# Clustered attention and two FFNs: the sums of v and of the weights in other products, b's abs at another place, a new order

## The chip, the cores and the metric

The kernel runs on one core of one Trainium2 chip. TensorE is PE here, its weight loads PEld, VectorE is DVE, ScalarE ACT, GpSimd POOL, and SyncE SP; SPq is SP's own queue, on which it issues DMAs. The metric is the device time of one execution in microseconds; the median over the runs is the time of a kernel.

## The reference

```python
q_n, k_n, c_n = q / (|q| + 1e-6), k / (|k| + 1e-6), centroids / (|centroids| + 1e-6)
q_assign = argmax(einsum('bhsd,hcd->bhsc', q_n, c_n)); k_assign = the same with k_n
scores = q @ k.T / sqrt(D), and -1e9 where q_assign != k_assign
attn = exp(scores - max); attn = attn / (sum(attn) + 1e-9)
x = (attn @ v) as 1536 tokens of 512
h = x @ w_in;  g = softplus(h);  x = g @ w_out             # first FFN, 512 -> 2048 -> 512
h = x @ w_in;  g = P(h) / (Q(h) + 1e-6);  out = g @ w_out  # second FFN
P = a0 + a1 h + a2 h^2 + a3 h^3;  Q = 1 + |b0| |h| + |b1| h^2
```

There are 2 batches, 8 heads, 768 positions, heads of 64 and 16 clusters. Everything is float32.

## The kernel before

**Attention.** A batch and two heads make a pair; there are eight pairs, 0 to 7. The two heads of a pair lie in one tile. `dots` (L231) multiplies x, which holds q and k, by the centroids, transposes on DVE (L237), and `onehot1` and `onehot2` (L244 to L255) find the best cluster. `mask_rows` scales the one-hot on ACT (L260) and SP moves it by eight DMAs of 16x384 into rows of the operands `qt` and `kt` (L148), so that the product of the scores has the mask in it. `split1` to `split4` cut q and k into a high and a low part, on ACT and DVE and with DMAs. `maxes` (L277, L281) are the products for the row maxima, twelve per pair, each reduced on DVE into a column of `mf`; `max_rows` (L289, L291) transposes `mf` on PE (`nt`), and a DMA puts the negated maxima into `qt` as one more row (`nr`). Then `scores` (L321, L322) makes twelve tiles `st` of 128 keys for 768 queries, ACT takes the exponential into `et` (L326), and from the second key tile on, POOL adds `et` up in `ea` (L331). `av` (L343) multiplies by v; `sums` (L366) multiplies `ea` by ones, so that every row of a head's 64 holds the sum; `evac_sums` and `finish` (L375 to L396) make the reciprocal with Ln, Exp and one correction on DVE, multiply and split the result into `xh` and `xl`. Since the mask leaves equal terms in rows, a small share of the sum of v is taken away: `vsum1` (L300) reduces v over the key tiles on DVE, `vsum2` (L306, L309) sums over partitions on PE (`vt`) into `nv`, the bias of `evac_av` (L357).

**Banks.** PSUM has three rotating bank pairs from `bank()`, for `st`, `mxs`, `dt`, `nt`, `vt` and `sm`, and one pair for `av`.

**Order.** `step(j)` issues the scores of pair j, the maxes of j+1, dots and splits of j+2 and the rest of j-1. The order on all engines comes from tables of positions: `AT` for a steady step, `S0` and `M0` for step 0, `LEAD` for what lies ahead of it, `DE` for the weight decode in steps 6 and 7, `FT` for the start of the FFN and the decode in the second. Functions are called in the sequence of their positions, and each engine works in that order.

**FFNs.** A unit is one chunk of 128 hidden features for 512 tokens: 12 products for h (L497 to L499) and 12 for yp (L568 to L574), each of three terms of a high and low split; 16 chunks, 3 blocks and 2 FFNs make 96 units. A weight chunk is decoded in five pieces: three on DVE (L429, L435, L441), a cast on ACT (L447), a subtraction on DVE (L450). The polynomial runs on ACT and DVE (L516 to L539), `gh` and `gl` are the two parts of its result, and the outputs `yo` leave PSUM by copies shared between DVE and ACT (L596, L597). `b_sb` holds b; its absolute value is taken in the lead (L678).

## Time and profile before

| | us |
|---|---|
| median of 3 runs (lowest to highest) | 816.33 (814.92 to 818.18) |
| the profiled execution, and its span | 817.65, 815.9 |
| PE busy in the span | 774.9 (95%) |
| DVE, ACT, POOL busy | 596.7, 443.2, 186.6 |
| the chain that ended last | PE 73%, DVE 15%, ACT 7%, DMA 2% |
| first score of pair 0, first `gl` product of the FFN | 46.55, 276.41 |

A row of a timeline gives the start in us, the duration, engine, line, operation, output and inputs, tile and count, and in brackets the idle time ahead of it and what released it. A window's row gives busy time of each engine with counts, then the granted clock of TensorE as a share of full speed, the DMA share and GB/s. The sums (`sm`) of pairs 4, 5, 6 and 7 begin at 185.8, 214.9, 245.1 and 267.1.

### The profile page before, as it was taken

The numbers are of one execution on the slowest core, as the hardware profiler recorded it, in microseconds if no ns is written. First come the engines' busy times: TensorE is split into PE (matmuls) and PEld (weight loads), VectorE is DVE, ScalarE is ACT, GpSimd is POOL, SyncE is SP. The second block draws the span as 40 slices with busy tenths as digits, with TensorE's granted clock in tenths as the row PEclk, the third lists the DMA queues.
The fourth block names the chain that finished last, engine by engine and source line by source line (L and its number), as shares of the span: only waits on it lengthen the run. The fifth ranks groups of instructions, "written<-read, shape, count | busy, mean of one in ns | idle before, by whom it ended". The sixth has DMA issues, their size and how long they took to land.

```text
span 815.9 us, 9120 instructions
## 1 busy us (share of the span) xinstructions
PE 774.9 (95%) x3468; PEld 573.9 (70%) x3468; DVE 596.7 (73%) x760; ACT 443.2 (54%) x626; POOL 186.6 (23%) x103
## 2 busy tenths in 40 slices
...
GB/s 185 166 46 128 132 146 81 112 125 62 123 71 239 320 41 1 104 0 1 1 1 0 104 197 171 200 104 0 1 1 0 52 1 0 1 0 53 1 1 51
DMA packets 14635, 61.65 MB, mean 76 GB/s; under 512 B 3248, under 2 KB 4368, under 8 KB 10496
## 3 DMA queue, kind: packets, MB, share of 16 engines
...
q8 instruction: 27, 0.44, 0.2%
...
## 4 chain that ended last, share of the span: by engine, by line
PE 73%; DVE 15%; ACT 7%; DMA 2%; issue 1%; POOL 1%; SPq 0%; ACTq 0%; POOLq 0%; DVEq 0%
PE h L498 9%; PE h L499 9%; PE h L497 9%; PE av L343 7%; PE yp L569 5%; PE yp L570 5%; PE yp L568 5%; PE st L321 4%; PE yp L572 4%; PE yp L573 4%; PE yp L574 4%; PE st L322 3%; PE mxs L277 3%; ACT et L326 2%; DVE y L531 2%; DVE y L539 2%
## 5 line engine op out<-in xcount | busy, mean ns | idle before, releaser
L498 PE MATMUL h<-xl,w 128*128 128x512 f32 x384 | 151.9, 396 | 0.0
L499 PE MATMUL h<-xh,w 128*128 128x512 f32 x384 | 151.8, 395 | 0.0
L497 PE MATMUL h<-xh,w 128*128 128x512 f32 x384 | 151.6, 395 | 0.0
L331 POOL TENSOR_TENSOR ea<-ea,et 128x768 f32<-128x768 f32 x60 | 118.3, 1989 | 26.0 <-ACT et L326 23.9
L553 DVE TENSOR_TENSOR gl<-y,gh 128x512 fp32r<-128x512 f32 x48 | 33.1, 690 | 116.7 <-ACT gh L545 116.7
L510 ACT ACTIVATE y<-h 128x512 f32<-128x512 f32 x48 | 28.8, 599 | 154.0 <-PE h L499 154.0
L281 DVE TENSOR_REDUCE mf<-mxs 128x1 f32<-128x768 f32 x96 | 87.7, 950 | 33.8 <-PE mxs L277 32.8
L326 ACT ACTIVATE et<-st 128x768 f32<-128x768 f32 x96 | 73.4, 812 | 71.1 <-PE st L322 68.1
L497 PEld LDWEIGHTS h<-xh,w 128*128 128x128 f32 x384 | 72.1, 188 | 17.9 <-issue 0.6
L498 PEld LDWEIGHTS h<-xl,w 128*128 128x128 f32 x384 | 72.1, 188 | 17.4
L499 PEld LDWEIGHTS h<-xh,w 128*128 128x128 f32 x384 | 72.0, 188 | 17.3
L572 PE MATMUL yp<-w,gh 128*128 128x512 f32 x192 | 75.7, 394 | 4.3 <-ACT gh L547 2.3
L569 PE MATMUL yp<-gl,w 128*128 128x512 f32 x192 | 76.9, 400 | 2.9 <-DVE gl L553 2.9
L568 PE MATMUL yp<-gh,w 128*128 128x512 f32 x192 | 76.5, 399 | 1.4 <-issue 1.4
L570 PE MATMUL yp<-gh,w 128*128 128x512 f32 x192 | 76.5, 399 | 0.0
L573 PE MATMUL yp<-w,gl 128*128 128x512 f32 x192 | 75.8, 395 | 0.5 <-DVE gl L555 0.5
L574 PE MATMUL yp<-w,gh 128*128 128x512 f32 x192 | 75.5, 393 | 0.0
L343 PE MATMUL av<-et,vr 128*64 128x384 f32 x384 | 73.0, 508 | 1.0 <-ACT et L326 1.0
L321 PE MATMUL st<-qt,kt 128*128 128x384 f32 x192 | 70.7, 368 | 2.8 <-DVE mf L281 2.1
L322 PE MATMUL st<-qt,kt 81*128 81x384 f32 x192 | 65.9, 343 | 0.0
L277 PE MATMUL mxs<-kt,qt 80*128 80x384 f32 x192 | 52.9, 385 | 11.3 <-DMA kt<-mr 4.8
L321 PEld LDWEIGHTS st<-qt,kt 128*128 128x128 f32 x192 | 36.8, 192 | 24.8 <-DVE mf L281 7.1
...
## 6 DMA issues: line engine op xcount, KB each, us to landing
...
rawx<-in_x SPq DMA_DIRECT2D x7, 768.0 KB, 6.5
rawy<-in_y SPq DMA_DIRECT2D x7, 768.0 KB, 6.4
...
```

Of the source, the lines that this page charges most:

```text
L321: nc.tensor.matmul(t[:, n, 0:HS], lhsT=KT[j % 3][:, 0, h, c], rhs=QT[j % 3][:, 0, h, r], start=True, stop=False)
L331: eng.tensor_tensor(out=ea[j, h], in0=et[j, 0, h] if kt == 1 else ea[j, h], in1=e, op=ALU.add)
L343: nc.tensor.matmul(av_t[j][64 * h:64 * h + 64, n, 0:HS], lhsT=VR[j % 2][:, h, kt, :], rhs=et[j, kt, h][:, n, :], start=kt == 0, stop=kt == ...
L497: nc.tensor.matmul(t, lhsT=wh[:, kk, :], rhs=h, start=kk == 0, stop=False)
L498: nc.tensor.matmul(t, lhsT=wh[:, kk, :], rhs=l, start=False, stop=False)
L499: nc.tensor.matmul(t, lhsT=wl[:, kk, :], rhs=h, start=False, stop=kk == KD - 1)
L568: nc.tensor.matmul(t, lhsT=wh[:, s], rhs=gh, start=first, stop=False)
L569: nc.tensor.matmul(t, lhsT=wh[:, s], rhs=gl, start=False, stop=False)
L570: nc.tensor.matmul(t, lhsT=wl[:, s], rhs=gh, start=False, stop=last)
L572: nc.tensor.matmul(t, lhsT=gh[:, s], rhs=wh, start=first, stop=False)
L573: nc.tensor.matmul(t, lhsT=gl[:, s], rhs=wh, start=False, stop=False)
L574: nc.tensor.matmul(t, lhsT=gh[:, s], rhs=wl, start=False, stop=last)
```

## The change

1. `vsum1` and `vsum2` are gone. A tile of `et` has one more column of ones; the value product of the second half has 385 columns, and the sum of v comes out in the last, which `evac_av` reads as its bias. `et` has eight fixed tiles instead of six that rotate.
2. The sums are taken in four column tiles of 32, in two rounds: first `ea`, then directly the last key tile, which POOL no longer adds. The reciprocal works on 384 columns instead of 768, and eight DMAs of 32x384 on SP spread it into `rr`.
3. `dots` multiplies by the raw centroids, which arrive transposed as one more input `ct`; an ACT activation (`scaled`) applies the reciprocal norm `rn`. The transpose on PE and the scaled copy are gone; the plain centroids come in eight small DMAs.
4. The absolute value of b is taken at step 2, and the DMAs of a and b are issued after both heads' maxima of pair 0.
5. All tables of positions are new, and the lead and step 0 are sorted as one sequence with a table of its own, `A0`. The load of the next x and y moves to the end of a step. At the start of the FFN one h group stands ahead of the last value product, and two stand between the last sums and the first yp; before, it was two and one.
6. In the second FFN the polynomial's `qr` has its own two buffers, all `yo` of blocks 0 and 1 are copied on ACT, the first yp of blocks 1 and 2 comes a unit later, and the decode of chunks 14 and 15 is spread out.

```diff
-AT = dict(S=[[0.31, 0.59, 2.52, 2.92, 2.56, 5.1], [0.23, 0.9, 2.82, 3.36, 2.83, 3.41]],
+AT = dict(S=[[0.28, 0.44, 2.19, 3.3, 2.6, 1.85], [0.2, 0.25, 2.53, 3.17, 2.8, 3.59]],
...
-    A=[-0.02, 0.22, 1.25], L=[0.26, 0.77, 1.61], D2=[[51.2, 51.8, 52.2, 52.4, 52.8], [56.2, 56.8, 57.2, 57.4, 57.8]])
+    A=[0.25, 1.03, 2.14], L=[0.86, 2.1, 2.52], D2=[[49.6, 51.0, 52.6, 53.15, 54.2], [55.5, 56.8, 58.2, 59.15, 59.5]])
...
+    ET = [ap_.tile([128, S + 1], F32, name=f"et{s}") for s in range(NE)]
...
-        nc.vector.transpose(t, d[:, 0, 0:HS])
+        nc.scalar.activation(out=u, in_=d[:, 0, 0:HS], func=AF.Identity, scale=rn[:, j % PB:j % PB + 1])
+        nc.vector.transpose(t, u)
...
-    def vsum1(j):
...
-    def vsum2(j):
...
     def scores(j, kt, h):
...
-        if kt:
+        if 0 < kt < NT - 1:
...
     def av(j, kt):
...
-                    av_t[j][64 * h:64 * h + 64, n, 0:HS], lhsT=VR[j % 2][:, h, kt, :], rhs=et[j, kt, h][:, n, :],
-                    start=kt == 0, stop=kt == NT - 1,
+                    av_t[j][64 * h:64 * h + 64, n, 0:HS + n], lhsT=VR[j % 2][:, h, kt, :],
+                    rhs=et[j, kt, h][:, n * HS:(n + 1) * HS + n], start=kt == 0, stop=kt == NT - 1,
...
-        nc.scalar.activation(out=t, in_=av_t.pop(j)[:, :, 0:HS], func=AF.Identity, scale=-1.0, bias=NV[j % 2])
+        p = av_t.pop(j)
+        nc.scalar.activation(out=NV[j % 2], in_=p[:, 1, HS:HS + 1], func=AF.Copy, scale=EPS / S)
+        nc.scalar.activation(out=t, in_=p[:, :, 0:HS], func=AF.Identity, bias=NV[j % 2])
...
     def sums(j):
...
-        for n in range(2):
+        for x in range(2):
             for h in range(2):
-                nc.tensor.matmul(
-                    t[64 * h:64 * h + 64, n, 0:HS], lhsT=ones, rhs=ea[j, h][:, n, :], start=True, stop=True
-                )
+                src = ea[j, h] if x == 0 else et[j, NT - 1, h]
+                for n in range(2):
+                    g = 32 * (2 * h + n)
+                    nc.tensor.matmul(
+                        t[g:g + 32, 0, 0:HS], lhsT=ones[:, 0:32], rhs=src[:, n * HS:(n + 1) * HS], start=x == 0, stop=x == 1
+                    )
...
-            nc.vector.scalar_tensor_tensor(out=r0, in0=w0, scalar=-2.0, in1=r0, op0=ALU.add, op1=ALU.mult)
+            nc.vector.scalar_tensor_tensor(out=r0, in0=w0, scalar=2.0, in1=r0, op0=ALU.add, op1=ALU.mult)
+            for h in range(2):
+                for n in range(2):
+                    g = 32 * (2 * h + n)
+                    for r in (64 * h, 64 * h + 32):
+                        nc.sync.dma_start(out=w[r:r + 32, n, :], in_=r0[g:g + 32, :])
         elif part == 3:
-            nc.vector.tensor_tensor(out=a, in0=a, in1=r0, op=ALU.mult)
+            nc.vector.tensor_tensor(out=a, in0=a, in1=w, op=ALU.mult)
...
-        qr = pools["wa"].tile([128, 2, TB], F32, tag="w32", name="qr", bufs=3)
+        qr = pools["wa"].tile([128, 2, TB], F32, tag="qr", name="qr", bufs=2)
...
-        nc.scalar.copy(y, t) if i % 2 else nc.vector.tensor_copy(y, t)
+        nc.scalar.copy(y, t) if i % 2 or blk < NB - 1 else nc.vector.tensor_copy(y, t)
...
-            nc.vector.scalar_tensor_tensor(out=b_sb, in0=b_sb, scalar=-1.0, in1=b_sb, op0=ALU.mult, op1=ALU.max)
...
-            for _, _, fn in sorted(seq, key=lambda x: x[:2]):
+            for _, _, fn in sorted(seq + lead, key=lambda x: x[:2]):
...
         for j in range(NP - 1):
+            if j == 2:
+                nc.vector.scalar_tensor_tensor(out=b_sb, in0=b_sb, scalar=-1.0, in1=b_sb, op0=ALU.mult, op1=ALU.max)
...
-            put(F1 + 0.8 + 0.01 * (i - F1) if F1 - 2 <= i < F1 else i + (1 + (c == 0), 3)[f] + 0.9, o)
+            put(F1 + 0.8 + 0.01 * (i - F1) if F1 - 2 <= i < F1 else i + (1 + (c == 0), 3 + (c == 0 and blk > 0))[f] + 0.9, o)
```

The order at three places. First DVE at the end of the lead, before; `mf_111` are the maxima of pair 0, `mf_112` those of pair 1, `nr` the negated maxima:

```order
L255 STREAM_TRANSPOSE oh<-turned 128x384
L281 TENSOR_REDUCE mf_111<-mxs 128x1 x4
L678 SCALAR_TENSOR_TENSOR b_sb<-b_sb 128x2
L281 TENSOR_REDUCE mf_111<-mxs 128x1
L291 TENSOR_SCALAR nr<-nt 6x128
L281 TENSOR_REDUCE mf_112<-mxs 128x1 x2
```

The same place of the changed kernel, where `mf_114` and `mf_115` are the maxima of pairs 0 and 1:

```order
L287 TENSOR_REDUCE mf_114<-mxs 128x1
L258 TENSOR_REDUCE dmx<-turned 128x24
L259 TENSOR_TENSOR turned<-iota,dmx 128x384
L261 STREAM_TRANSPOSE oh<-turned 128x384
L287 TENSOR_REDUCE mf_114<-mxs 128x1 x4
L297 TENSOR_SCALAR nr<-nt 6x128
L287 TENSOR_REDUCE mf_115<-mxs 128x1 x2
```

The absolute value of b no longer stands among the maxima.

Second SP's queue in a steady step, before; `mr` are mask rows, `nr` the maxima's row, `qt` and `kt` the operands:

```order
L148 DMA qt_105<-nr 1x12x128
L145 DMA vr_110<-in_v 128x768
L148 DMA kt_107<-qt_104 16x1536
L148 DMA kt_107<-qt_104 48x1536
L148 DMA kt_107<-kt_107 64x1536
L148 DMA qt_104<-qt_104 16x1536
L140 DMA rawx<-in_x 128x1536
L140 DMA rawy<-in_y 128x1536
L148 DMA qt_104<-mr 16x384 x2
L148 DMA kt_107<-mr 16x384 x2
```

The same queue of the changed kernel, from one `nr` to the mask rows behind it:

```order
L152 DMA qt_100<-nr 1x12x128
L144 DMA rawx<-in_x 128x1536
L144 DMA rawy<-in_y 128x1536
L149 DMA vr_113<-in_v 128x768
L152 DMA kt_102<-qt_99 16x1536
L152 DMA kt_102<-qt_99 48x1536
L152 DMA qt_99<-qt_99 16x1536
L418 DMA rr<-r_869 32x384 x8
L152 DMA kt_102<-kt_102 64x1536
L152 DMA qt_99<-mr 16x384 x2
L152 DMA kt_102<-mr 16x384 x2
```

The loads of x and y now stand right behind `nr`, and the eight DMAs of the reciprocal stand ahead of the last key copy and the mask rows.

Third DVE in step 6, before; `mf_112` are the maxima of pair 7, and `w` the pieces of the first weight chunk:

```order
L291 TENSOR_SCALAR nr<-nt 12x128
L281 TENSOR_REDUCE mf_112<-mxs 128x1 x4
L429 TENSOR_SCALAR w_1790<-w_1770 128x1024
L435 SCALAR_TENSOR_TENSOR w_1790<-w_1770,w_1790 128x1024
L281 TENSOR_REDUCE mf_112<-mxs 128x1 x2
L441 SCALAR_TENSOR_TENSOR w_1790<-w_1770,w_1790 128x1024
L300 TENSOR_REDUCE vs<-vr_110 128x128
L281 TENSOR_REDUCE mf_112<-mxs 128x1
L450 TENSOR_TENSOR w_1849<-w_1790,w_1849 128x1024
```

The same step of the changed kernel, where `mf_115` are pair 7's maxima:

```order
L297 TENSOR_SCALAR nr<-nt 12x128
L287 TENSOR_REDUCE mf_115<-mxs 128x1 x8
L411 TENSOR_TENSOR sm<-sm,r_1799 128x384
L413 SCALAR_TENSOR_TENSOR r_1799<-sm,r_1799 128x384
L287 TENSOR_REDUCE mf_115<-mxs 128x1 x3
L420 TENSOR_TENSOR avs<-avs,rr 128x768
L287 TENSOR_REDUCE mf_115<-mxs 128x1
L459 TENSOR_SCALAR w_1932<-w_1759 128x1024
L297 TENSOR_SCALAR nr<-nt 12x128
L465 SCALAR_TENSOR_TENSOR w_1932<-w_1759,w_1932 128x1024
L471 SCALAR_TENSOR_TENSOR w_1932<-w_1759,w_1932 128x1024
```

All twelve maxima of pair 7 now precede the first piece of a weight.

## Rows read from the trace of the kernel before

**Rows 1.** Windows: a steady step, three slow stretches, one h group; busy by engine, clock.

```profile
106.39:132.84 26.45, 26.12 (x141) 15.97 (x143) 21.71 (x26) 18.16 (x23) 23.27 (x12) 1.00 0.42 116
214.00:218.00 4.00, 4.00 (x14) 1.60 (x13) 3.07 (x3) 1.83 (x3) 2.26 (x2) 0.57 0.02 4
229.00:240.00 11.00, 8.28 (x29) 3.44 (x27) 8.32 (x7) 1.25 (x4) 8.36 (x4) 0.69 0.00 1
268.53:271.30 2.77, 2.77 (x14) 2.18 (x12) 2.70 (x4) 2.60 (x3) 0.00 (x0) 1.00 0.52 186
277.00:282.00 5.00, 5.00 (x13) 3.94 (x12) 4.01 (x5) 4.95 (x6) 0.00 (x0) 0.50 1.02 426
```

**Rows 2.** Timeline of the lead, ACT, SP's queue, DVE and PE, 34.8 to 47.2.

```profile
34.88 0.71 ACT L260 ACTIVATE mr<-oh,msc 128x384 fp32r<-128x384 f32 x1 [5.93 <-DVE oh L255]
...
36.24 1.16 SPq L148 DMA_DIRECT2D qt<-mr  x2
...
40.87 1.22 SPq L148 DMA_DIRECT2D kt<-mr  x2
...
45.37 0.16 DVE L678 SCALAR_TENSOR_TENSOR b_sb<-b_sb 128x2 f32<-128x2 f32 x1 [7.09 <-DMA b_sb<-in_moe_b]
...
46.55 0.66 PE L321 MATMUL st<-qt,kt 128*128 128x384 f32 x1
```

**Rows 3.** Timeline of PE in steps 5 and 6.

```profile
213.70 0.44 PE L321 MATMUL st<-qt,kt 128*128 128x384 f32 x1 [2.10 <-DVE mf L281]
...
214.92 2.80 PE L366 MATMUL sm<-ea,ones 128*64 128x384 f32 x8
...
232.18 1.01 PE L277 MATMUL mxs<-kt,qt 80*128 80x384 f32 x2 [2.44 <-DVE mf L281]
...
240.68 1.51 PE L343 MATMUL av<-et,vr 128*64 128x384 f32 x8 [0.96 <-ACT et L326]
```

**Rows 4.** Timeline of PE at the start of the FFN.

```profile
273.04 0.47 PE L568 MATMUL yp<-gh,w 128*128 128x512 f32 x1 [1.44 <-issue]
...
276.41 0.79 PE L569 MATMUL yp<-gl,w 128*128 128x512 f32 x1 [2.89 <-DVE gl L553]
```

**Rows 5.** Timeline of PE in a steady step, 106.3 to 133.

```profile
106.32 1.51 PE L366 MATMUL sm<-ea,ones 128*64 128x384 f32 x8
...
108.31 0.85 PE L231 MATMUL dt<-rawx,cc 128*32 128x384 f32 x8
...
122.26 0.38 PE L306 MATMUL vt<-ones,vs 128*128 128x1 f32 x2
...
124.97 0.87 PE L277 MATMUL mxs<-kt,qt 80*128 80x384 f32 x4
```

**Rows 6.** Timelines of DVE and PE in the second FFN, two stretches.

```profile
569.83 1.23 DVE L450 TENSOR_TENSOR w<-w,w 128x1024 fp32r<-128x1024 f32 x1 [1.11 <-ACT w L447]
...
573.76 0.49 PE L572 MATMUL yp<-w,gh 128*128 128x512 f32 x1 [1.55 <-ACT gh L547]
...
644.89 0.47 PE L572 MATMUL yp<-w,gh 128*128 128x512 f32 x1 [2.00 <-DVE yo L596]
```

**Rows 7.** Timeline of ACT in the same steady step.

```profile
107.92 0.90 ACT L375 ACTIVATE sm<-sm,eps 128x768 f32<-128x768 f32 x1
...
126.66 1.47 ACT L154 CAST qt<-rawx 128x1536 fp32r<-128x1536 f32 x1
```

**Rows 8.** Timeline of SP's queue in the same steady step.

```profile
114.02 0.58 SPq L140 DMA_DIRECT2D rawx<-in_x  x1
...
122.50 1.22 SPq L148 DMA_DIRECT2D kt<-mr  x2
```

**Rows 9.** The page's DMA issues: count, KB each, us from issue to landing.

```profile
rawx<-in_x SPq DMA_DIRECT2D x7, 768.0 KB, 6.5
```

**Rows 10.** Timeline of DVE in step 6: pieces of the first weight chunk.

```profile
210.04 2.73 DVE L435 SCALAR_TENSOR_TENSOR w<-w,w 128x1024 uint32<-128x1024 uint32 x1
...
214.43 1.21 DVE L441 SCALAR_TENSOR_TENSOR w<-w,w 128x1024 uint32<-128x1024 uint32 x1
```

210 lines of the change are left out of this document (116 added, 94 removed).

## Prediction

> **What bounds the kernel now.** I read the windows first. A steady step of the attention takes 26.45 us and PE is busy for 26.12 of them, while DVE has 21.71, ACT 18.16 and POOL 23.27 [rows 1]. So in these steps only work on PE, or a wait of PE, is worth time, and shorter work on DVE, ACT or POOL is worth nothing by itself. Three more windows of that group show a granted clock of 0.57, 0.69 and 0.50. The timelines say what came just before. In the lead, DVE waits 7.09 us for a DMA, and PE's first score with it [rows 2]. In steps 5 and 6 two waits of PE, of 2.10 and 2.44 us, end on a DVE maximum [rows 3], and at the start of the FFN there are two of 1.44 and 2.89 us [rows 4]. After such a wait matmuls take twice as long for some microseconds: the sums of pair 5 take 2.80 us [rows 3] where those of a steady pair take 1.51 [rows 5]. So a wait costs itself and then a stretch at the lower of TensorE's two levels. In the FFNs PE is almost without gaps; those that count are in the second one [rows 6].
>
> The sum is made against the profiled execution, 817.65 us, which is 1.32 above the median of 816.33.
>
> **The lead: minus 4.5.** The first score is queued on PE behind the transpose `nt` of head 1's maxima. That waits for the last maximum, and this one stands on DVE behind the absolute value of `b_sb`, which sat 7.09 us for a DMA that SP issued behind eight mask-row DMAs [rows 2]. The change puts that instruction at step 2, where its data landed long ago. Then the next late thing decides: pair 1's mask rows, since two maxes of pair 1 now stand ahead of the first score. The rows of head 0 are issued by about 38.7 (the eight run from 36.24 to 42.09 and the first four are head 0's) and I let them land 2 us later, an estimate. The path to them gets longer: centroids come in eight more small DMAs, and an ACT activation `scaled` of 128x384 is put in; the mask activation of that shape took 0.71 [rows 2], so I add 0.85 to 1. The first score then comes at 42.0 instead of 46.55, minus 4.5. The ends are minus 7 (the whole wait goes) and minus 2 (the norm of the centroids, behind the late DMAs, holds `scaled`). The two maxes that now run before the first score are work taken out of what follows: 0.87 for two of them [rows 5], of which I count 0.7.
>
> **The steady steps.** PE loses `vt`, 0.38 busy at most [rows 5]; since ends are modelled, I take 0.25. The extra column in the value product is one in 385 and costs nothing that I can see. The sums become two rounds of four 32-column products. The nearest row is the dots, which already are four column tiles: 0.85 [rows 5]. Two rounds are 1.70, against 1.51 for the sums now: plus 0.19, of which I take 0.15. Net minus 0.1 in each of eight pairs: minus 0.8, with ends of minus 3.0 (0.38 each) and plus 1.5 (0.19 each).
>
> The Trainium skill speaks against column tiles as a full gain ("TensorE: Matmul & The Clock Gate", section "Why this matters for your kernels"): three tiles of 32 columns ran 2.38 times as fast as one after the other, not three times. By that, an estimate, four tiles would give 3.2 and the two rounds some 1.8 us, 0.25 more in each pair, 2 us in all; the row of the dots shows four tiles at no such loss, and the sum above goes by that row.
>
> Off PE, DVE loses the sum over v and half of two passes, POOL two of its ten additions, and ACT half of the sums' evacuation, 0.90 now [rows 7], and gains `scaled`. By the windows none of these is the bound, so I count nothing. What they buy is slack, and two things eat it. First, the reciprocal now goes through eight DMAs on SP, queued ahead of the last key copy and of the next pair's eight mask rows. Two mask rows took 1.22 to issue [rows 8], so eight are 4.9 us. Today the last mask row is issued by 123.72, 1.25 before the maxes at 124.97 that come next [rows 5, 8], so there is no room on today's order; the new order moves the one-hot earlier and lets the maxes start later, and by laying these durations along it I find 1.5 us left. DVE itself then waits about 1.4 us at avs times `rr`, with one maximum queued behind it and PE's `nt` behind that; there DVE has its slack. Second, the load of x and y moves from the middle of a step (issued at 114.02, used at 126.66 by the cast) to its end, behind the move of the maxima [rows 7, 8]. Landing takes 6.5 us [rows 9]. Issued 24.6 us into a step of 26.4, x lands 4.7 into the next, and the cast of 1.47 then ends at about 6.2, in front of the evacuation of the sums, which could go at 5.5. Behind it on ACT stand four exponentials and the evacuation that frees the only av bank pair. I take 0.3 for each of six steps, plus 1.8; the ends are minus 3 (bank waits shrink with the lighter DVE) and plus 8.
>
> **Steps 5 to 7 and the start of the FFN: minus 8.1.** Before, the first weight pieces stand between the maxima on DVE: 2.73 us for one of them [rows 10]. PE waits for their banks. Waits that go: 2.10, 2.44 and 0.96 [rows 3], 1.44 and 2.89 [rows 4], together 9.8. The clock that goes with them: 4.00 us at 0.57, 8.28 busy at 0.69 and 5.00 at 0.50 [rows 1] are 1.7, 2.6 and 2.5, together 6.8. In all 16.6. In the new order all twelve maxima of pair 7 precede the first piece, and two FFN groups instead of one lie between the last sums and the first yp: twelve products take 2.77 [rows 1], so 5.5 us, against which stand two evacuations, a table load, softplus, cast and gl. I put these at some 5.2, an estimate: before, the first yp came 273.04 - 268.53 = 4.5 after one group began, and gl's own subtraction comes on top [rows 1, 4]. What is late next: the first decoded chunks. Their casts stand on ACT ahead of the evacuation of the sums of pair 6 and of avs, and each waits for three DVE pieces that only start now. Three pieces, of 2.73 and 1.21 and one like the shorter, are 5.2 after the last maximum [rows 10], while PE has about 4.2 us of queued work there (three groups of eight at 1.51 [rows 5], less their overlap); I take 2.0 for the first, 3.5 for the second, which holds the av banks, 2.5 for the clock after them and 0.5 at the first yp: 8.5. So minus 8.1. The ends are minus 16 (none of it shows) and minus 2.
>
> **The second FFN: minus 4.5.** The decode of chunks 14 and 15 stands on DVE in front of the polynomial, and DVE idles 1.11 for its cast; PE then waits 1.55 for gh [rows 6]. The second of the two chunks gives a wait of the same kind. Together that is between 1.55 and twice as much, and I take 2.8. Spread over more units, and with `qr` in buffers of its own, they go. The wait of 2.00 for `yo` on DVE [rows 6] goes because ACT now copies all four and the first yp comes a unit later. I leave 0.3 for ACT. Ends: minus 2 and minus 5.1.
>
> The rest (`ET` in fixed slots, memsets, the norm's arithmetic) lies on engines with slack, or in the lead inside its bounds.
>
> **Sum.** -4.5 - 0.7 - 0.8 + 1.8 - 8.1 - 4.5 = -16.8, so 800.85 for an execution like the profiled one, and 799.5 for the median.
>
> **Rivals.**
> A. Faster, but the new order costs more in the steps: x lands later than I think, or ACT's evacuation of avs holds the av banks by 1.2 us in each of six steps instead of 0.3. That is 5.4 more: 805. For it: ACT's chain in front of the av banks is the tightest place of the new order. Against it: ACT is busy for only 18 of 26 us. Chance 0.21.
> B. No change: the late loads cost 3 us a step, 16 more than I count, and the rest comes as forecast: 815. It needs x to land 3 us later than 6.5 after issue. Chance 0.09.
> C. Slower: the eight `rr` DMAs hold the mask rows. If the issue of 4.9 us on SP comes in full in front of the next pair's first maxes, six steps lose 29 us, 799.5 + 29 = 828. It decides from where the last mask row lands after these maxes are due; to end slower it has to take about 4 us of every step. For it: today's margin is 1.25 us. Against it: the mask rows come earlier in the new order. Chance 0.07.
> D. Faster than forecast: the stalls on the first chunks don't show, 8 less: 791.5. It is inside the forecast's own ends.
>
> **How the numbers follow.** The forecast with D has 0.63. It holds 790 to 803. The range takes in A and the ends of the lead: 789 to 811. About 0.5% (4.1 us) is what a measurement of this kernel can tell from no change, so faster means below 812.2: the forecast, A, little of B, 0.84. Same 0.09, slower 0.07.
>
> **What would show it.** The first score at 42 and no DVE wait on `b_sb`. A steady step between 26 and 27 us, sums of about 1.6 us, no `vt`. No wait of PE for a maximum in steps 5 and 6, a granted clock of 1.00 there, and a wait of avs's bank in step 7. The first yp less than 1 us after the third h group. No gap over 0.5 in the second FFN. I am wrong if SP's mask rows are what PE's first maxes of a step wait for, or if the cast of x holds ACT by more than 1 us a step.

## The result, and the profile after

The changed kernel takes 808.95 us in the median of four runs (808.54 to 809.76), the kernel before 817.25 on the same occasions: a ratio of 0.9903, with a 95% interval of 0.9877 to 0.9929. That is 8.3 us, half of the 16.8 that were forecast. The profiled execution took 808.61, its span is 806.8. Where the 9.1 us of the two spans lie is read at landmarks that have the same work of PE ahead of them. The first score of pair 0 is no such landmark: it starts at 47.05 instead of 46.55, where 42.0 was forecast, but two maxes of pair 1 stand ahead of it now. The transposes `nt` of the maxima of pairs 1 and 6 are. Their rows in the kernel before, then in the changed one:

```profile
70.56 0.28 PE L289 MATMUL nt<-ident,mf 128*12 128x128 f32 x1
...
201.99 0.27 PE L289 MATMUL nt<-ident,mf 128*12 128x128 f32 x1
```

```profile
69.25 0.28 PE L295 MATMUL nt<-ident,mf 128*12 128x128 f32 x1
...
202.96 0.27 PE L295 MATMUL nt<-ident,mf 128*12 128x128 f32 x1 [0.28 <-DVE mf L287]
```

| us | before | after | difference | forecast |
|---|---|---|---|---|
| start to `nt` of pair 1 | 70.56 | 69.25 | -1.31 | -5.2 |
| from there to `nt` of pair 6 | 131.43 | 133.71 | +2.28 | +1.0 |
| from there to the first `gl` product of the FFN | 74.42 | 69.54 | -4.88 | -8.1 |
| first `gl` product to the end | 539.49 | 534.30 | -5.19 | -4.5 |

The first forecast is -4.5 and -0.7, the second -0.8 and +1.8. At `nt` of pair 6 the new order has one score tile more behind it, four products or 0.7 us; with the same work the second difference is +1.6 and the third -4.2. The lead of the kernel before reaches `nt` of pair 1 at 70.56 in one run and at 72.40 in another (that of the decode's order below), so the first difference is known to some 2 us only. Inside the second stretch the four steps from pair 0's sums to pair 4's took 26.81 us each (75.24 to 182.48) instead of 26.48 (79.89 to 185.82), so 1.3 us more, where the forecast allowed about 0.8. By the profile's busy time of PE in them (104.96 against 104.30 us), half of the 1.3 is work and half is idle time.

The lead is the surprise. Its timeline (start, duration, engine, line, operation, tile; in brackets the idle time before and what ended it), which answers to [rows 2]:

```profile
1.21 3.58 ACTq L643 DMA_DIRECT2D craw<-in_centroids  x4
...
1.66 4.32 SPq L643 DMA_DIRECT2D craw<-in_centroids  x4
...
8.96 0.42 DVE L673 TENSOR_TENSOR csq<-craw 128x256 f32<-128x256 f32 x1 [4.45 <-DMA craw<-in_centroids]
...
12.65 0.58 ACT L242 ACTIVATE scaled<-dt,rn 128x384 f32<-128x384 f32 x1 [2.13 <-DVE rn L684]
...
17.51 0.71 ACT L266 ACTIVATE mr<-oh,msc 128x384 fp32r<-128x384 f32 x1 [1.37 <-DVE oh L261]
...
40.38 1.16 SPq L152 DMA_DIRECT2D qt<-mr  x2
...
45.64 1.62 PE L283 MATMUL mxs<-kt,qt 80*128 80x384 f32 x4 [4.31 <-DMA kt<-mr]
...
47.05 0.52 PE L319 MATMUL st<-qt,kt 128*128 128x384 f32 x1
```

The wait for `b_sb` is gone, yet the first score is no earlier than before. The eight DMAs of the centroids keep ACT's and SP's queues for 3.58 and 4.32 us, four on each, and the DMAs of y and of the next x queue behind them. DVE's first instruction of the norm waits for them until 8.96; `scaled` waits for the norm, and pair 0's mask activation comes at 17.51, 3.54 later than the 13.97 of before. From there all is late: the mask rows of pair 1 start at 40.38 instead of 36.24, the maxes that stand ahead of the first score wait 4.31 us for them, and the score follows.

The windows (busy time of the engines, then the granted clock, DMA share and GB/s) of two stretches of the lead and of the start of the FFN, which answer to [rows 1]:

```profile
40.00:44.00 4.00, 0.27 (x1) 0.08 (x1) 1.28 (x3) 1.47 (x1) 0.00 (x0) 0.87 0.88 340
44.00:50.00 6.00, 4.36 (x14) 4.39 (x15) 2.69 (x3) 0.96 (x2) 0.00 (x0) 0.52 0.33 79
270.60:280.00 9.40, 7.97 (x22) 6.10 (x23) 7.13 (x8) 9.02 (x11) 0.00 (x0) 0.64 1.01 427
```

After the idle stretch the lead runs at 0.52, and the start of the FFN at 0.64. Timeline of PE, which answers to [rows 3 to 6]:

```profile
102.01 0.85 PE L384 MATMUL sm<-ea,ones 128*32 128x384 f32 x8
...
102.68 0.83 PE L384 MATMUL sm<-et,ones 128*32 128x384 f32 x8
...
232.47 0.85 PE L384 MATMUL sm<-ea,ones 128*32 128x384 f32 x8 [1.28 <-POOL ea L331]
...
241.44 4.21 PE L354 MATMUL av<-et,vr 128*64 128x384 f32 x16 [3.04 <-ACT avs L371]
...
270.60 0.47 PE L598 MATMUL yp<-gh,w 128*128 128x512 f32 x1 [3.53 <-issue]
...
272.50 0.80 PE L599 MATMUL yp<-gl,w 128*128 128x512 f32 x1 [1.43 <-DVE gl L583]
...
638.73 0.50 PE L602 MATMUL yp<-w,gh 128*128 128x512 f32 x1 [0.45 <-ACT yo L626]
```

The sums take 0.85 and 0.83 for their two rounds. In step 7, PE waits 3.04 for avs's evacuation, as forecast in kind (3.5). The 1.28 ahead of it is another wait than the 2.0 that was forecast for the first chunk: it ends on POOL, whose five additions of `ea` run from 221.29 to 232.42 without a break. And the first yp waits 3.53 and its gl product 1.43, where 0.5 was forecast. In the second FFN the largest wait left is 0.45. Timeline of ACT behind the last value product, where the first yp's reason stands:

```profile
266.41 1.05 ACT L477 CAST w<-w 128x1024 fp32r<-128x1024 f32 x1 [2.16 <-DVE w L471]
...
269.93 0.57 ACT L399 ACTIVATE last<-sm,eps 128x384 f32<-128x384 f32 x1
```

The evacuation of the last sums (L399, 269.93) stands behind a weight cast that waits 2.16 for DVE, a table load, a softplus and `gh`. The first yp starts 0.1 us after that evacuation ends; that it waits for the bank pair of these sums is shown by a run below. Before, the evacuation came directly behind that of the value product. Last, the queue and DVE in a steady step, which answer to [rows 8]:

```profile
112.55 5.91 SPq L418 DMA_DIRECT2D rr<-r  x8
...
120.08 1.95 DVE L420 TENSOR_TENSOR avs<-avs,rr 128x768 f32<-128x768 f32 x1 [1.73 <-DMA rr<-r]
```

The eight DMAs of the reciprocal take 5.91 us to issue in this step and 4.94 to 5.25 in the six others (4.9 were reckoned). DVE waits 1.73 for them here, and 0.80 to 1.94 in five steps, 1.28 in the mean (1.4 were reckoned). The cast of x, which the prediction watched too, does wait for its late load: ACT idles 7.52, 7.33, 6.67 and 6.54 us ahead of it in four steps.

### The profile page after: what moved, and what is told of

It reads as the page before. It is cut to its first block, busy times and chain, and to the rows that moved or that the text cites. A ratio compares the mean times of both kernels' runs of the same rounds, so it can differ in the third digit from the quotient of the medians.

```text
span 806.8 us, 9354 instructions
## 1 busy us (share of the span) xinstructions
PE 770.4 (95%) x3522; PEld 570.8 (71%) x3523; DVE 581.8 (72%) x745; ACT 439.4 (54%) x638; POOL 153.9 (19%) x97
## 4 chain that ended last, share of the span: by engine, by line
PE 65%; DVE 17%; ACT 5%; issue 4%; SPq 4%; DMA 3%; POOL 2%; DVEq 0%; ACTq 0%; POOLq 0%
PE h L529 8%; PE h L527 8%; PE h L528 8%; PE yp L599 5%; PE yp L600 5%; PE yp L598 5%; PE av L354 4%; PE yp L602 4%; PE yp L603 4%; PE yp L604 4%; PE st L319 3%; SPq L152 3%; PE mxs L283 2%; PE st L320 2%; SPq L418 1%
## 5 line engine op out<-in xcount | busy, mean ns | idle before, releaser
L331 POOL TENSOR_TENSOR ea<-ea,et 128x768 f32<-128x768 f32 x46 | 92.6, 2032 | 17.0 <-ACT et L325 15.9
L354 PE MATMUL av<-et,vr 128*64 128x385 f32 (+1 forms) x384 | 72.6, 505 | 3.3 <-ACT avs L371 3.0
L283 PEld LDWEIGHTS mxs<-kt,qt 80*128 80x128 f32 x192 | 33.5, 199 | 31.7 <-issue 17.3
```

The lines of the kernel that those rows point to most:

```text
L283: nc.tensor.matmul(t[:, n, 0:HS], lhsT=QT[j % 3][0:RM, 0, h, i * 128:(i + 1) * 128], rhs=KT[j % 3][0:RM, 0, h, n * HS:(n + 1) * HS], start ...
L354: nc.tensor.matmul(av_t[j][64 * h:64 * h + 64, n, 0:HS + n], lhsT=VR[j % 2][:, h, kt, :], rhs=et[j, kt, h][:, n * HS:(n + 1) * HS + n], st ...
```

## The experiments

All times are medians of four to ten runs, beside the kernel before in the same rounds (816.6 to 817.3). The changed kernel's 808.95 comes from other rounds, and single runs of one kernel are 1 to 6.5 us apart; a difference of 1 or 2 us to it counts only where the profile shows it at a landmark as well.

### The absolute value of b alone

On the kernel before, the one instruction moved from the lead to step 2, and the DMAs of a and b put behind the maxima of pair 0 (`AB`):

```diff
-    AB=20.21, B0=20.08, B=[2.33, -3.64, 11.46, 17.3, 22.94], BN=[6.44, 6.2, 7.15, 6.15, 5.61])
+    AB=27.12, B0=20.08, B=[2.33, -3.64, 11.46, 17.3, 22.94], BN=[6.44, 6.2, 7.15, 6.15, 5.61])
...
-            nc.vector.scalar_tensor_tensor(out=b_sb, in0=b_sb, scalar=-1.0, in1=b_sb, op0=ALU.mult, op1=ALU.max)
+            if j == 2:
+                nc.vector.scalar_tensor_tensor(out=b_sb, in0=b_sb, scalar=-1.0, in1=b_sb, op0=ALU.mult, op1=ALU.max)
```

> The kernel before with one edit: the absolute value of b is taken at step 2 and the DMAs of a and b go behind the maxima of pair 0. Theory 1 (DVE's wait for b held PE's first score, and pair 1's mask rows are late next, by about 42 to 44 us): first scores at about 38.5, then a shorter wait of PE at pair 1's first maxes, and 3 to 5 us less in all, about 813. Theory 2 (the mask rows would have held PE until then anyway): the wait reappears in full at these maxes and the time falls by 1 us or less, 816 to 817.

807.65 against 816.61, a ratio of 0.9899 (0.9870 to 0.9928): 9.0 us, twice what theory 1 expected, and as much as the whole change. Timeline of PE, windows of the two stretches, and the window of the kernel before at its first scores:

```profile
39.57 0.63 PE L321 MATMUL st<-qt,kt 128*128 128x384 f32 x1
...
41.62 0.94 PE L277 MATMUL mxs<-kt,qt 80*128 80x384 f32 x4 [0.19 <-DMA qt<-mr]
...
62.63 0.28 PE L289 MATMUL nt<-ident,mf 128*12 128x128 f32 x1
```

```profile
40.00:44.00 4.00, 3.81 (x20) 3.07 (x19) 1.99 (x4) 2.11 (x3) 1.64 (x1) 1.00 0.14 29
44.00:50.00 6.00, 5.80 (x33) 3.58 (x32) 5.52 (x7) 4.30 (x6) 5.68 (x4) 1.00 0.26 66
```

```profile
46.50:50.00 3.50, 3.50 (x12) 3.50 (x13) 0.28 (x1) 1.32 (x2) 0.00 (x0) 0.50 0.24 63
```

In this order the first two score tiles (eight products) stand ahead of pair 1's maxes, so they start at 39.57 and cover the landing of the mask rows: the maxes then wait 0.19 us. PE stays busy and the clock is 1.00 in both windows, where the changed kernel has 0.87 and 0.52. The first score is 7.0 us earlier and `nt` of pair 1 7.9 (62.63 instead of 70.56). So the wait hid no other one, and it was worth more than its own length, since the kernel before ran its first scores at 0.50.

### The lead of the changed kernel

One DMA for the plain centroids instead of eight, from an input `cr` that holds them in the tile's layout, made outside the kernel:

```diff
-        for h in range(2):
-            for b in range(4):
-                r = 64 * h + 16 * b
-                both[b % 2].dma_start(out=craw[r:r + C], in_=cent.rearrange("(p h) c d -> h c p d", h=2)[h])
+        nc.sync.dma_start(out=craw.rearrange("p a d -> p (a d)"), in_=cr)
```

> The changed kernel with one edit: the plain centroids arrive by one DMA of 128x256, laid out with their copies beforehand, instead of eight small DMAs. Theory 1 (the norm of the centroids, late behind the eight DMAs, holds the lead): the first mask activation of pair 0 comes about 3 us earlier than 17.51, the first score at about 44 instead of 47.05, and the time falls by 3 us, to about 806. Theory 2 (SP's own queue of moves and loads holds pair 1's mask rows, the norm only looks late): the first score stays within 0.5 us of 47.05 and the time does not move, 809.

807.56 (806.09 to 809.14), 1.4 below the changed kernel, between the two theories; `nt` of pair 1 comes at 68.01, 1.2 earlier. Timelines of SP's queue, ACT and PE:

```profile
1.66 0.43 SPq L641 DMA_DIRECT2D craw<-in_cr  x1
...
15.40 0.71 ACT L267 ACTIVATE mr<-oh,msc 128x384 fp32r<-128x384 f32 x1 [1.37 <-DVE oh L262]
...
44.03 1.62 PE L284 MATMUL mxs<-kt,qt 80*128 80x384 f32 x4 [4.43 <-DMA kt<-mr]
```

The issue falls from 4.32 to 0.43 and the mask activation comes 2.1 us earlier, but PE still waits 4.43 for pair 1's mask rows. So the eight DMAs were 2.1 of the 3.54 by which that activation was late, and the order on PE keeps the wait whatever the norm does.

The first scores ahead of pair 1's maxes:

```diff
-    M=[47.3, 25.52, 36.45, 24.32, 31.76, 39.41, 39.76, 44.37, 48.32, 47.44, 47.45, 31.24],
+    M=[47.3, 31.26, 36.45, 31.25, 31.76, 39.41, 39.76, 44.37, 48.32, 47.44, 47.45, 31.24],
```

> The changed kernel with one edit: the two maxes of pair 1 that stand ahead of the first score on PE go behind the first four scores (positions 31.25 and 31.26 instead of 24.32 and 25.52). Theory 1 (PE's order makes the scores wait for pair 1's mask rows, though they need none of them): the first score starts at about 41.4 instead of 47.05, right behind the transpose of the last maxima, the wait for the mask rows shrinks to about 1 us, and the time falls by 3 to 4 us, to about 805.5. Theory 2 (the mask rows are the real limit, and what runs ahead of them is given back later): the wait moves behind the scores and the time stays within 1 us of 809.

807.52 (807.1 to 809.2), between the two theories. The first score comes at 41.62, 5.4 us earlier; of that 0.6 is left at `nt` of pair 1 (68.63) and 1.4 in the median. Windows:

```profile
41.50:46.00 4.50, 4.48 (x17) 4.38 (x17) 1.24 (x2) 3.51 (x4) 0.55 (x1) 0.62 0.58 203
50.00:55.00 5.00, 5.00 (x19) 3.00 (x18) 4.62 (x5) 3.51 (x5) 2.88 (x2) 0.50 0.10 42
```

The granted clock is 0.62 under the first scores and 0.50 a while later: PE had been idle for 1.98 us before them. Much of what began earlier ran at the lower level.

Both edits together:

```diff
+        nc.sync.dma_start(out=craw.rearrange("p a d -> p (a d)"), in_=cr)
...
+    M=[47.3, 31.26, 36.45, 31.25, 31.76, 39.41, 39.76, 44.37, 48.32, 47.44, 47.45, 31.24],
```

> The changed kernel with the two edits of the lead together: plain centroids in one DMA, first scores ahead of pair 1's maxes. Theory 1 (the lead holds most of the 5 us that the other parts cost): the sums of pair 0 start at about 72 instead of 75.2 and all of it stays to the end, 805 to 806. Theory 2 (the earlier lead is given back at the start of the FFN, as in the run with all three edits): 807 to 808.

806.82 (806.43 to 807.43), 2.1 below the changed kernel and between the two theories. Pair 0's sums come at 73.70, not at the 72 of theory 1; and theory 2's reason isn't borne out, since the first gl product is 2.1 earlier as well. Timeline of PE and a window:

```profile
43.01 0.44 PE L320 MATMUL st<-qt,kt 128*128 128x384 f32 x1 [1.09 <-ACT et L326]
...
44.79 2.37 PE L284 MATMUL mxs<-kt,qt 80*128 80x384 f32 x6 [0.80 <-DMA kt<-mr]
...
67.72 0.27 PE L296 MATMUL nt<-ident,mf 128*12 128x128 f32 x1
```

```profile
44.00:52.00 8.00, 7.21 (x26) 5.55 (x26) 5.43 (x5) 3.28 (x5) 7.00 (x4) 0.56 0.21 54
```

The first scores start at 39.50, as early as in the run with b's abs alone. Then a score waits 1.09 for the exponentials and the maxes 0.80 for the mask rows, and the clock is 0.56 from 44 to 52 and 0.59 from 52 to 56. In the run with b's abs alone it is 1.00 from 40 to 55. By `nt` of pair 1 this run is 5.1 us behind that one (67.72 against 62.63). The busy time at the lower clock, 7.21 and 4.00 us, is 3.2 and 1.6 us more than it would be at 1.00, an estimate, which is nearly all of it. What PE did ahead of the first score differs: the filler products of the lead (`busy`, which only keep PE busy) end at 39.71 in the run with b's abs alone, and here at 36.97, with an idle time of 1.74 us ahead of the scores. No run fills that gap, so that the clock is what the lead lost is argued and not shown.

### The late load and the DMAs of the reciprocal

```diff
-    MR=4.19, SP=[-13.16, -0.12, 0.23, 2.32, 1.74], LD=5.12, LV=-0.46)
+    MR=4.19, SP=[-13.16, -0.12, 0.23, 2.32, 1.74], LD=0.5, LV=-0.46)
```

> The changed kernel with one edit: the load of the next x and y goes back to an early place in the step (position 0.5 instead of 5.12). Theory 1 (the late load makes the steady steps 0.35 us longer than before, since the cast of x waits for it ahead of the sums' evacuation): the steps from one sum to the next fall from 26.8 to about 26.3 us, the time falls by 2 to 3 us, to about 806.5. Theory 2 (the steps are longer for another reason: the reciprocal's DMAs, the sums in column tiles, the new order of maxes): the steps stay at 26.6 to 26.9 us and the time at 809.

810.42 (809.51 to 812.68), not faster; the steps took 27.34, 26.68, 26.68 and 27.95. Theory 1 falls: without the wait for the load, the two steps of 26.68 are no shorter than those of the changed kernel (26.59 to 27.29). In the two longer ones the first maxes wait 0.62 and 0.95 for mask rows, a cost of the early load that neither theory had.

```diff
-    AV0=-2.06, EV=1.58, SM=-0.22, ES=-0.1, LN=1.55, W=[1.68, 2.07, 3.3], XH=4.96, D=1.72, E1=2.13, E2=2.95, OT=3.13,
+    AV0=-2.06, EV=1.58, SM=-0.22, ES=-0.1, LN=1.55, W=[1.68, 2.07, 4.25], XH=4.96, D=1.72, E1=2.13, E2=2.95, OT=3.13,
```

> The changed kernel with one edit: avs times rr goes behind the last maximum and nr on DVE (position 4.25 instead of 3.3). Theory 1 (the eight DMAs of the reciprocal end late, DVE waits 1.7 us for them with the last maximum queued behind, and PE's transpose of the maxima waits for that): this wait of PE, 0.4 us a step, goes, the steps fall from 26.8 to 26.4 and the time by 2 us, to 807. Theory 2 (the transpose would be held anyway, by the maxes' own rate on DVE): steps and time stay.

812.55 (812.03 to 814.49), 3.6 slower; the steps took 27.0 to 27.3. Timeline of DVE around the maxima:

```profile
124.40 2.44 DVE L420 TENSOR_TENSOR avs<-avs,rr 128x768 f32<-128x768 f32 x1
...
126.76 5.47 DVE L287 TENSOR_REDUCE mf<-mxs 128x1 f32<-128x768 f32 x6
```

The wait for `rr` is gone, but the product of 2.44 us now stands in front of the next pair's six maxima, and PE's maxes wait for these in three of the steps, 0.92, 0.87 and 0.63. Both theories fall. DVE's wait of 1.73 was there, and it cost less where it stood.

### The start of the FFN

Softplus, gh and gl of the first unit ahead of the next decode:

```diff
-    A=[0.25, 1.03, 2.14], L=[0.86, 2.1, 2.52], D2=[[49.6, 51.0, 52.6, 53.15, 54.2], [55.5, 56.8, 58.2, 59.15, 59.5]])
+    A=[0.2, 1.03, 2.14], L=[0.21, 2.1, 2.52], D2=[[49.6, 51.0, 52.6, 53.15, 54.2], [55.5, 56.8, 58.2, 59.15, 59.5]])
```

> The changed kernel with one edit: at the start of the FFN the first softplus, gh and gl stand ahead of the next weight chunk's decode on ACT and DVE (positions 0.2 and 0.21 instead of 0.25 and 0.86). Theory 1 (the cast of that chunk, ordered ahead of the softplus, makes the first yp late): the first yp starts at about 267.5 instead of 270.6 and its gl product follows without a wait, the low clock after it is shorter, and the time falls by 4 to 5 us, to about 804.5. Theory 2 (the evacuation of the last value product, which waited for POOL, sets the start): at most 1 us is gained, 808.

811.37 (810.78 to 811.8), 2.4 slower. Timelines of ACT and PE:

```profile
269.38 0.58 ACT L399 ACTIVATE last<-sm,eps 128x384 f32<-128x384 f32 x1
...
270.05 0.47 PE L598 MATMUL yp<-gh,w 128*128 128x512 f32 x1 [3.33 <-issue]
...
279.25 0.80 PE L599 MATMUL yp<-gl,w 128*128 128x512 f32 x1 [4.38 <-DVE gl L583]
```

`gh` is ready at 266.5, yet the first yp starts at 270.05, right behind the evacuation of the sums: this shows the bank as the reason. And the gl product of the second unit waits 4.38. So that evacuation was moved as well, in two forms:

```diff
-FT = dict(G=[-3.8, -0.95, 0.53], AV=-1.15, SM=-0.98, EV=[-0.65, 0.8], FN=[1.81, 2.53, 3.5, 5.51, 7.39],
-    A=[0.25, 1.03, 2.14], L=[0.86, 2.1, 2.52], D2=[[49.6, 51.0, 52.6, 53.15, 54.2], [55.5, 56.8, 58.2, 59.15, 59.5]])
+FT = dict(G=[-3.8, -0.95, 0.53], AV=-1.15, SM=-0.98, EV=[-0.65, -0.6], FN=[1.81, 2.53, 3.5, 5.51, 7.39],
+    A=[0.2, 1.03, 2.14], L=[0.21, 1.04, 2.15], D2=[[49.6, 51.0, 52.6, 53.15, 54.2], [55.5, 56.8, 58.2, 59.15, 59.5]])
```

> The changed kernel with one edit: at the start of the FFN the evacuation of the last sums stands right behind that of the last value product on ACT, as in the kernel before (position -0.6 instead of 0.8), ahead of softplus, and the first two softplus, gh and gl stand ahead of the next chunks' decode. Theory 1 (the first yp waits for the bank of these sums, whose evacuation stood behind a weight cast, a table load and a softplus): the first yp starts at about 267.3 instead of 270.6, with no wait over 1 us for the next gl, the clock stays at 1.00, and the time falls by 5 to 6 us, to about 803.5. Theory 2 (the decode on DVE limits the start, the bank only looks late): the first yp comes earlier, and a wait of the same length appears within three units; the time stays within 1.5 us of 809.

806.92 (806.17 to 808.81), 2.0 below the changed kernel. The first yp starts at 267.41 as expected, but the gl product of the second unit waits 3.35: theory 2's wait, at a time between the two theories. The second form moves the second unit's gh and gl as well:

```diff
-    A=[0.2, 1.03, 2.14], L=[0.21, 1.04, 2.15], D2=[[49.6, 51.0, 52.6, 53.15, 54.2], [55.5, 56.8, 58.2, 59.15, 59.5]])
+    A=[0.2, 0.212, 2.14], L=[0.205, 0.214, 2.15], D2=[[49.6, 51.0, 52.6, 53.15, 54.2], [55.5, 56.8, 58.2, 59.15, 59.5]])
```

> The changed kernel with the sums' evacuation at -0.6 as in the run before it, and both first softplus, gh and gl directly behind it, ahead of all further weight pieces. Theory 1 (in the run with one softplus ahead, PE waited 3.3 us for the second gl, which stood behind six weight pieces on DVE; the start needs the bank and both gl): the first yp at 267.4, no wait over 1 us up to unit 4, the clock at 1.00 there, and the time falls by 5 to 6 us, to about 803.5. Theory 2 (DVE has more decode to do in this stretch than time, whatever stands first): the wait moves to a later product of units 2 to 4, and the time stays at 806 to 808.

810.52 (809.99 to 811.78), 1.6 slower than the changed kernel. Timelines of PE and ACT:

```profile
282.92 0.80 PE L598 MATMUL yp<-gh,w 128*128 128x512 f32 x1 [6.58 <-ACT gh L575]
...
275.58 1.05 ACT L477 CAST w<-w 128x1024 fp32r<-128x1024 f32 x1 [4.41 <-DVE w L471]
```

The first yp comes at 267.17 with a wait of 0.31, the second unit has none over 0.3, and the third waits 6.58 for its gh: ACT stands 4.41 us in front of a cast whose pieces DVE now does later, and behind it come three table loads, two for the last pair's reciprocal and one back to softplus. The wait has moved twice and grown. This is theory 2, at a time worse than it expected: DVE's decode holds PE through the order of the instructions on ACT.

This second form together with the two edits of the lead, that is the one DMA of the centroids and the first scores ahead of pair 1's maxes:

> The changed kernel with three edits together: the plain centroids in one DMA, the first scores ahead of pair 1's maxes, and the start of the FFN of the run before. Theory 1 (three separate losses): they add up, 1.4 + 1.4 + 5.5, to about 800.5. Theory 2 (the lead's two are one loss, since earlier scores only wait at a lower clock for the same mask rows): 1.4 + 5.5, to about 802.

807.64 (806.7 to 809.1), and both theories fall. The three edits bring the first gl product to 263.96 instead of 272.50; the run before had it at 267.91, so 4.0 of the 8.5 are the lead's. At the third unit the same wait of 6.58 takes most of it back.

### The order of the decode

On the kernel before, the first pieces behind all maxima of pair 7:

```diff
-    [-11.88, -5.68, -3.02, -3.84, -4.46],
-    [-2.84, 0.47, 3.51, -4.55, 4.5],
+    [-1.9, -1.7, -1.5, -1.3, -0.9],
+    [-1.1, 0.47, 3.51, -0.8, 4.5],
```

> The kernel before with one edit: the first weight pieces go behind all maxes of pair 7 on DVE (seven positions of the decode table in step 6), as in the changed kernel. Theory 1 (the pieces between the maxima cost step 5 and 6 their waits and the clock after them, and later decode has room): the waits of 2.10 and 2.44 us and the low clock behind them vanish, 7 to 9 us less by the sums of pair 6, of which 3 or so come back in step 7; 811 to 812 in all. Theory 2 (the decode only moves the stall: chunks come as much later as the maxima come earlier, and PE waits in step 7 and at the start of the FFN): what is gained by pair 6's sums is lost again by the first yp, 815 to 818.

820.18, a ratio of 1.0054 (1.0030 to 1.0078), slower. Timelines of PE and ACT:

```profile
237.50 2.83 PE L343 MATMUL av<-et,vr 128*64 128x384 f32 x8 [5.18 <-ACT et L326]
...
246.07 0.69 PE L321 MATMUL st<-qt,kt 128*128 128x384 f32 x1 [2.62 <-ACT et L326]
...
244.27 1.04 ACT L447 CAST w<-w 128x1024 fp32r<-128x1024 f32 x1 [6.10 <-DVE w L441]
```

The waits of 2.10 and 2.44 are gone, as theory 1 has it, and two of 5.18 and 2.62 have come, each for an exponential that stands on ACT behind a cast which waits for its pieces (5.63 and 6.10). Theory 2, and worse than it.

On the changed kernel, the tables of the decode and of the start of the FFN as before:

```diff
-    [-12.4, -6.53, -3.05, -4.1, -5.1],
-    [-2.61, 1.83, 1.41, -1.2, 0.04],
...
+    [-11.88, -5.68, -3.02, -3.84, -4.46],
+    [-2.84, 0.47, 3.51, -4.55, 4.5],
...
-FT = dict(G=[-3.8, -0.95, 0.53], AV=-1.15, SM=-0.98, EV=[-0.65, 0.8], FN=[1.81, 2.53, 3.5, 5.51, 7.39],
-    A=[0.25, 1.03, 2.14], L=[0.86, 2.1, 2.52], D2=[[49.6, 51.0, 52.6, 53.15, 54.2], [55.5, 56.8, 58.2, 59.15, 59.5]])
+FT = dict(G=[-8.44, -11.09, 1.12], AV=-5.78, SM=-1.04, EV=[-1.36, -0.96], FN=[0.66, 1.12, 3.35, 5.33, 9.13],
+    A=[-0.02, 0.22, 1.25], L=[0.26, 0.77, 1.61], D2=[[49.6, 51.0, 52.6, 53.15, 54.2], [55.5, 56.8, 58.2, 59.15, 59.5]])
```

> The changed kernel with the tables of the weight decode and of the start of the FFN put back to those of the kernel before (the second FFN's part and everything else stay). Theory 1 (the new decode order and start are worth the 8 us that the forecast gave them): 815 or more, with the waits of step 5 and 6 back. Theory 2 (they only moved the stalls): 807 to 811.

810.36 (806.38 to 810.59), by 1.4 slower in the median and not clearly so. Timeline of PE at the start of the FFN:

```profile
275.42 0.80 PE L599 MATMUL yp<-gl,w 128*128 128x512 f32 x1 [3.02 <-DVE gl L583]
```

The old waits are back at this place, 1.21 for the first yp and 3.02 for its gl, where the changed kernel has 3.53 and 1.43. In steps 5 to 7 the 2.10 and 2.44 that theory 1 named don't come back; there are waits of 0.77, 1.67, 0.67, 0.78 and 1.72. Theory 2.

### The second FFN

The changed kernel with this part undone:

```diff
-        qr = pools["wa"].tile([128, 2, TB], F32, tag="qr", name="qr", bufs=2)
+        qr = pools["wa"].tile([128, 2, TB], F32, tag="w32", name="qr", bufs=3)
-        nc.scalar.copy(y, t) if i % 2 or blk < NB - 1 else nc.vector.tensor_copy(y, t)
+        nc.scalar.copy(y, t) if i % 2 else nc.vector.tensor_copy(y, t)
...
-            put(F1 + 0.8 + 0.01 * (i - F1) if F1 - 2 <= i < F1 else i + (1 + (c == 0), 3 + (c == 0 and blk > 0))[f] + 0.9, o)
+            put(F1 + 0.8 + 0.01 * (i - F1) if F1 - 2 <= i < F1 else i + (1 + (c == 0), 3)[f] + 0.9, o)
...
-    A=[0.25, 1.03, 2.14], L=[0.86, 2.1, 2.52], D2=[[49.6, 51.0, 52.6, 53.15, 54.2], [55.5, 56.8, 58.2, 59.15, 59.5]])
+    A=[0.25, 1.03, 2.14], L=[0.86, 2.1, 2.52], D2=[[51.2, 51.8, 52.2, 52.4, 52.8], [56.2, 56.8, 57.2, 57.4, 57.8]])
```

> The changed kernel with the second FFN's part undone: shared buffers of the polynomial, yo copied on DVE and ACT in turn, the first yp of a block at its old unit, and the decode of chunks 14 and 15 close together. Theory 1 (this part is worth what the forecast gave it and does not depend on the attention): the waits of 1.55, 0.76 and 2.00 us come back and the time rises by 4.5 to 5.5 us, to about 814. Theory 2 (part of the gain from the first yp to the end is clock at the start of the FFN, not the second FFN): it rises by 3 us or less.

815.71 (813.59 to 816.52), 6.8 more than the changed kernel, and 0.9987 of the kernel before (0.9972 to 1.0003): without this part the change is no gain that can be measured. Timeline of PE:

```profile
570.12 0.49 PE L602 MATMUL yp<-w,gh 128*128 128x512 f32 x1 [1.61 <-ACT gh L577]
...
599.56 0.50 PE L602 MATMUL yp<-w,gh 128*128 128x512 f32 x1 [0.69 <-ACT gh L577]
...
641.23 0.53 PE L602 MATMUL yp<-w,gh 128*128 128x512 f32 x1 [2.17 <-DVE yo L626]
```

Window behind the last of these waits:

```profile
640.00:645.00 5.00, 3.77 (x10) 2.98 (x11) 3.64 (x6) 2.43 (x5) 0.00 (x0) 0.66 0.56 210
```

All three waits are back, near the 1.55 and 2.00 of [rows 6] and the 0.76 between them. They and the shorter ones of 0.2 behind two of them come to 4.9. Behind the last, 3.77 busy us run at 0.66, some 1.3 more than at 1.00, an estimate; the kernel before has 1.00 from 645 to 650, behind its wait of 2.00. From the first activation of the polynomial to the end this run takes 280.1 us, the changed kernel 273.5 and the kernel before 278.8: the part itself is worth 5.2, and the other 1.3 is as much as that clock. Theory 1, and somewhat more.

### The two parts that pay, without the others

The kernel before with b's abs at step 2 and the spread decode, yo on ACT and the later first yp of the second FFN:

```diff
+            if j == 2:
+                nc.vector.scalar_tensor_tensor(out=b_sb, in0=b_sb, scalar=-1.0, in1=b_sb, op0=ALU.mult, op1=ALU.max)
+        nc.scalar.copy(y, t) if i % 2 or blk < NB - 1 else nc.vector.tensor_copy(y, t)
...
+            put(F1 + 0.8 + 0.01 * (i - F1) if F1 - 2 <= i < F1 else i + (1 + (c == 0), 3 + (c == 0 and blk > 0))[f] + 0.9, o)
...
+    A=[-0.02, 0.22, 1.25], L=[0.26, 0.77, 1.61], D2=[[49.6, 51.0, 52.6, 53.15, 54.2], [55.5, 56.8, 58.2, 59.15, 59.5]])
```

> The kernel before with two parts of the change alone: the absolute value of b at step 2, and of the second FFN the spread decode, yo on ACT and the later first yp, with the polynomial still in shared buffers. Theory 1 (these two hold all the gain of the change, and its other parts take some of it back): 9.0 from the first and 5 to 6.8 from the second, so 801 to 803, 6 us or more below the changed kernel. Theory 2 (the spread decode needs the polynomial's own buffers): the waits on gh stay, only the 2 us of yo are gained, and the time is about 805.5.

803.88 (803.53 to 804.84), a ratio of 0.9837 (0.9806 to 0.9869): 13.4 us below the kernel before and 5.1 below the changed one. This is the version that beats both. It falls 0.9 short of theory 1's range, and theory 2 falls: no wait on gh comes back. Timeline of PE at the start of the FFN:

```profile
267.65 0.79 PE L569 MATMUL yp<-gl,w 128*128 128x512 f32 x1 [2.90 <-DVE gl L553]
```

The wait for gl stands as before; in the second FFN 0.34, for `yo` at 633.61, is the largest left, with the polynomial still in shared buffers.

Two trials to take the wait for gl away, on top:

```diff
-    A=[-0.02, 0.22, 1.25], L=[0.26, 0.77, 1.61], D2=[[49.6, 51.0, 52.6, 53.15, 54.2], [55.5, 56.8, 58.2, 59.15, 59.5]])
+    A=[-0.02, 0.22, 1.25], L=[-0.01, 0.77, 1.61], D2=[[49.6, 51.0, 52.6, 53.15, 54.2], [55.5, 56.8, 58.2, 59.15, 59.5]])
```

> The kernel before with b's abs at step 2, the second FFN's part, and the first gl of the FFN ahead of the weight piece on DVE that waits for its cast (position -0.01 instead of 0.26). Theory 1 (the wait of 2.9 us for gl and the low clock behind it come from this order alone): the first gl product starts at about 265 instead of 267.7, and the time falls by 3 to 5 us from 803.9, to about 800. Theory 2 (DVE's decode limits the start): the wait comes back within three units, 803 to 805.

```diff
-    A=[-0.02, 0.22, 1.25], L=[-0.01, 0.77, 1.61], D2=[[49.6, 51.0, 52.6, 53.15, 54.2], [55.5, 56.8, 58.2, 59.15, 59.5]])
+    A=[-0.02, 0.22, 1.25], L=[-0.01, 0.23, 1.61], D2=[[49.6, 51.0, 52.6, 53.15, 54.2], [55.5, 56.8, 58.2, 59.15, 59.5]])
```

> As the run before it, and the second gl as early too (position 0.23 instead of 0.77). Theory 1 (each gl of the first units is late by the pieces ahead of it): 1 us less than that run, by the wait at the second unit. Theory 2 (decode limits): not faster than that run, and a longer wait at units 2 to 4.

805.96 (802.6 to 808.15) and 808.8 (805.52 to 812.0). Timeline of PE in the first trial, in its fastest run:

```profile
261.95 0.50 PE L569 MATMUL yp<-gl,w 128*128 128x512 f32 x1 [0.27 <-DVE gl L553]
...
269.14 0.50 PE L569 MATMUL yp<-gl,w 128*128 128x512 f32 x1 [2.59 <-DVE gl L553]
```

The first gl waits 0.27, and 7 us later the next one waits 2.59. Neither is faster in the median, and the runs are too far apart to say more.

## Why the prediction was wrong

**The range held, the size did not.** The sign and the places were right, and 808.95 lies inside the range; the sum was twice the result. Two steps failed, and they are of one kind: a wait was taken off the list without asking what the new order puts in its place.

**The lead (-4.5 and -0.7, measured -1.3 at `nt` of pair 1).** The step that failed is "so I add 0.85 to 1" for the path to pair 1's mask rows. They came 4.1 later. The row behind the term was one activation; pair 0's mask activation alone came 3.54 later, and 2.1 of that are the eight small DMAs, which were named and not priced and took about 1 us each to issue. The prediction put the norm behind late DMAs as its end of minus 2, so the mechanism was seen, and the size was not. Two smaller terms were short as well: the maxes began 2.8 after head 0's last mask row was issued (42.80 to 45.64), where 2 was taken, and the two maxes took 1.4 ahead of the first score, for which 42.0 left almost nothing. And the gain of the edit itself was underestimated: alone it is worth 9.0, since the scores cover the mask rows in the old order and the clock stays at 1.00. At `nt` of pair 1 that is 7.9, of which the changed kernel keeps 1.3. That two maxes of pair 1 stand ahead of the first score is a small part of this: putting the scores first gave 0.6 there.

**Steps 5 to 7 and the start of the FFN (-8.1, measured -4.9, or -4.2 with the same work).** The waits of [rows 3] did go, and the wait for avs's bank came as named, 3.04 against 3.5. The 2.0 ahead of it did not come as named; a wait of 1.28 for POOL stands near it. What failed is "0.5 at the first yp": the waits there are 3.53 and 1.43, and behind them 7.97 busy us run at 0.64. In the kernel before the same place had 1.44, 2.89 and 5.00 us at 0.50, and the sum counted all of that as gone. The 5.2 us of work on ACT before gl left out that the sums' evacuation had been put last in it, and that a cast waits in it. With the old tables in the changed kernel the stretch from `nt` of pair 6 to the first gl product takes 71.5 us, against 69.5 with the new and 74.4 before, so some 2 of the 4.9 belong to the new tables and the rest to the other parts. The runs with other orders of decode and start say why it is so little: DVE's pieces, ACT's casts and table loads and PE's first units hang together in order, and each edit left a wait at another place, three times a longer one (4.38, 6.58 and 5.18).

**The second FFN (-4.5).** Right in kind, and somewhat small: 5.2, and 6.8 when undone, with a lower clock behind the last wait.

**The steady steps (+0.2 each with all terms, measured +0.3).** The number is nearly right, and partly by luck. The sums' two rounds are 1.68 against the bound of 1.70, but PE's busy time rose by 0.17 a step, where -0.1 was forecast with `vt` gone. The +0.3 for the late load of x is not what the rest is: ACT did idle 6.5 to 7.5 us for it, a sign of being wrong that the prediction had named, and yet the run with the early load has no shorter step. The Trainium skill ("TensorE: Matmul & The Clock Gate", section "Why this matters for your kernels") measured 2.38 times for three column tiles, from which 1.8 was an estimate for four; the rows here say 1.68, so four tiles lost less than that. The issue of the eight `rr` DMAs and DVE's wait for them came out near the 4.9 and 1.4. Rival C did not come: the largest wait of these steps' maxes for mask rows is 0.17, at 125.74. Rival B did not come either, since the early load gave nothing.

**What stays open.** The two paying parts give 13.4 us and the whole 8.3, so the others cost 5.1 together. Beside the run of the two parts alone, the changed kernel is 7.5 later at `nt` of pair 1 (69.25 against 61.72), loses 2.3 more up to `nt` of pair 6, and wins 5.0 from there to the first gl product. So it is the rest of the lead that costs, and the start of the FFN that pays some of it back. Of the lead's 7.5 its two edits together brought back 1.5, and 3.4 in the run that had the start's edit as well. For what is left the profiles offer the lower clock between 44 and 56 us; no run took it away by itself, so that is argued and not shown.
